# Attention and FFN over half batches, Q and K in rows of three tokens, score units issued in pairs, masks per head pair

## Chip, cores and metric

One core of one Trainium2 chip. The metric is the device time of one execution in microseconds, and medians of several runs are quoted. "Span" is the time from the first to the last instruction in the profile; a run lies some 2 us above its span. The engines are PE (TensorE, matmul), DVE (VectorE), ACT (ScalarE), POOL (GpSimd) and SP (which issues the loads).

## The reference

Four batches, eight heads, 768 tokens, head dimension 64. Heads 0, 2 and 6 are full causal heads. The others see 4 sink tokens and a window of 64. The attention output, 3072 tokens by 512, goes through an FFN.

```python
scores = scale * np.matmul(q, k.transpose(0, 1, 3, 2))        # per batch and head, 768 x 768
mask = causal if retrieval head else causal & (sink | in_window)
a = softmax(where(mask, scores, -1e9))
x = (a @ v) laid out as [B * S, H * D]                        # 3072 x 512
h = np.maximum(np.maximum(x @ w1, x @ w2), x @ w3)            # 3072 x 768
out = h @ w_out                                               # 3072 x 512
```

## The kernel before

It walks over 16 head pairs (two heads, one whole batch of 768 tokens each). For a pair it casts Q and K to 16 bits, transposes them on PE into one PSUM tile, copies them to SBUF, and computes scores in six units. ACT takes the exponential and POOL multiplies by masks. A pair later PE multiplies by V, DVE normalises, and PE transposes the result to become the FFN's input. FFN work for a finished batch is dealt out in small portions ("fill") among the attention of the next batch.

```python
trp = tc.tile_pool(name="trp", bufs=1, space=PSUM)       # ONE transpose buffer
fsp = tc.tile_pool(name="fsp", bufs=2, space=PSUM)       # FFN accumulators
# ... cut ...
retr_row = ...                                           # is_retrieval, one partition
nc.gpsimd.partition_broadcast(out_ap=RT[:, 0:H], in_ap=retr_row[0:1, 0:H])
for h in range(H):                                       # all masks, at the start
    for c, (f, w) in ((0, (full, win)), (256, (full, win)), (512, (full0, win0))):
        nc.vector.scalar_tensor_tensor(out=mk[:, h, c : c + 256], in0=f,
            scalar=RT[:, h : h + 1], in1=w, op0=ALU.mult, op1=ALU.add)
# ... cut ...
def turn(src, nm):                                       # Q or K: [token, dim] -> [dim, token]
    tr = trp.tile([P, 1024], FP16, tag="tr", name="tr")
    for sb in range(NSB):
        nc.tensor.transpose(tr[:, sb * P : (sb + 1) * P],
                            src[:, sb].rearrange("p h d -> p (h d)"), ident)
    t = qkt.tile([P, S], FP16, tag=nm, name=nm)
    nc.vector.tensor_copy(out=t, in_=tr[:, 0:S])
    return t
# turn_x does the same with the normalised output x, into xT, through the same buffer
# ... cut ...
for i in range(NP + 1):
    # ...
    for u in range(6):
        scores(i, u, *cur)                               # conditions cut
        # u = 0..3: av(p, ...) and norm(p, ...) of the pair before
        # u = 2 and u = 4: turn_x(p, 0), turn_x(p, 1)
        # u = 3: nxt[0] = turn(qn, "QT")     u = 5: nxt[1] = turn(kn, "KT")
        fill(RATE)                                       # two FFN units after every score unit
```

Each use of the one transpose buffer is followed by FFN matmuls before the next use.

The softmax here doesn't subtract the row's maximum and nothing guards it: scores larger than these inputs give would overflow.

## Time and profile before

| | before |
|---|---|
| median, range (three runs) | 264.18 us, 261.42 to 264.54 |
| span | 259.6 us |
| first FFN matmul (yy) | 70.8 us |
| stage with attention and FFN | 70.8 to about 226 us |
| FFN alone | about 33.6 us |

The page of the kernel before, its second part: each digit is a tenth of busy time in one fortieth of the span.

```profile
PE   0004675785699999999999999999999999999993
POOL 2006999997997777777677868595959552000000
```

The same in numbers, busy time of each engine by stage (a stretch, its length, then busy time and number of instructions for PE, PE's weight loads, DVE, ACT and POOL, the granted clock, the DMA share and GB/s):

```profile
0.00:70.80 70.80, 33.25 (x318) 19.26 (x319) 43.42 (x81) 25.50 (x28) 49.42 (x59) 1.00 1.23 207
70.80:226.00 155.20, 154.84 (x1502) 85.03 (x1499) 98.78 (x204) 88.44 (x125) 107.86 (x116) 1.00 0.36 80
226.00:259.60 33.60, 29.46 (x155) 14.69 (x152) 11.34 (x21) 8.29 (x16) 0.00 (x0) 1.00 0.13 47
```

Before 70.8 us PE waits. From there it is busy 154.8 of 155.2 us, and at the end the FFN runs alone. The chain of waits (start, length, what) in this stretch of the middle stage is PE alone. Transposes ("tr"), then FFN ("yy"), then the next work: scores ("st") and products with V ("oacc").

```profile
83.71 0.17 PE tr L337 x3
83.88 1.30 PE yy L187 x8
85.18 0.27 PE st L273 x2
85.45 0.58 PE oacc L309 x15
86.03 0.34 PE tr L253 x6
86.36 1.30 PE yy L187 x8
```

The copies that empty the transpose buffer, from the groups of instructions (line, engine, operation, output from input, shapes, count, busy us and mean ns, idle time before):

```profile
L258 DVE COPY KT<-tr 128x768 f16<-128x768 f16 x16 | 8.9, 558 | 5.1 <-PE tr L253 4.3
L341 DVE COPY xT<-tr 128x384 f16<-128x384 f16 x32 | 11.4, 358 | 24.9 <-PE tr L337 24.9
```

So 768 contiguous elements take 0.56 us and 384 take 0.36.

### The profile page before, as it was taken

The numbers are of one execution on the slowest core, as the hardware profiler recorded it, in microseconds if no ns is written. First come the engines' busy times: TensorE is split into PE (matmuls) and PEld (weight loads), VectorE is DVE, ScalarE is ACT, GpSimd is POOL, SyncE is SP. The second block draws the span as 40 slices with busy tenths as digits, with TensorE's granted clock in tenths as the row PEclk, the third lists the DMA queues.
The fourth block names the chain that finished last, engine by engine and source line by source line (L and its number), as shares of the span: only waits on it lengthen the run. The fifth ranks groups of instructions, "written<-read, shape, count | busy, mean of one in ns | idle before, by whom it ended". The sixth has DMA issues, their size and how long they took to land.

```text
span 259.6 us, 4937 instructions
## 1 busy us (share of the span) xinstructions
PE 217.5 (84%) x1968; PEld 119.0 (46%) x1968; DVE 153.5 (59%) x305; ACT 122.2 (47%) x169; POOL 157.3 (61%) x174
## 2 busy tenths in 40 slices
PE   0004675785699999999999999999999999999993
PEld 0003252444355545554555555455645555554541
DVE  1497547675667656774678476847684563551550
ACT  1002744453656575647564756575556654223212
POOL 2006999997997777777677868595959552000000
PEclk9999999999999999999999999999999999999999
DMA  8999999999920079309920991030002001102003
GB/s 152 218 218 218 218 217 195 202 202 218 218 38 0 3 163 260 66 3 185 263 42 3 205 263 20 3 121 3 0 24 102 3 0 71 53 0 93 31 0 121
DMA packets 80344, 28.62 MB, mean 110 GB/s; under 512 B 74946, under 2 KB 77250, under 8 KB 80322
## 3 DMA queue, kind: packets, MB, share of 16 engines
q1 hardware_dynamic: 77954, 25.17, 49.5%
q0 software_dynamic: 2368, 3.15, 6.8%
q8 instruction: 15, 0.25, 0.4%
q14 instruction: 7, 0.06, 0.1%
HBM read 25.17 MB, written 6.29 MB: 121 GB/s over the span
## 4 chain that ended last, share of the span: by engine, by line
PE 69%; DVE 10%; POOL 9%; SPq 5%; DMA 2%; issue 2%; ACT 0%; DVEq 0%; ACTq 0%; POOLq 0%
PE yy L187 34%; PE yo L205 12%; PE oacc L309 9%; PE st L273 7%; POOL pt L284 5%; SPq L103 5%; PE tr L253 4%; DVE qn L234 3%; PE tr L337 3%; POOL vf L240 3%; DMA qs<-in_q_dram 2%; DVE kn L235 2%; DVE va L238 2%; POOL vf L244 1%; DVE acc L198 1%
## 5 line engine op out<-in xcount | busy, mean ns | idle before, releaser
L280 ACT ACTIVATE pt<-st 128x1024 f16<-128x1024 f32 (+1 forms) x96 | 87.4, 919 | 69.9 <-PE st L273 67.1
L284 POOL TENSOR_TENSOR pt<-pt,mk 128x512 f16<-128x512 f16 (+2 forms) x96 | 103.3, 1100 | 23.1 <-ACT pt L280 23.0
L240 POOL TENSOR_SCALAR vf<-va,RT 128x325 f16<-128x325 f16 x32 | 35.5, 1108 | 29.3 <-DVE va L238 27.9
L198 DVE TENSOR_TENSOR acc<-yy,acc 128x384 f16<-128x384 f32 x48 | 26.8, 558 | 37.9 <-PE yy L187 33.2
L195 ACT CAST acc<-yy 128x384 f16<-128x384 f32 x48 | 23.0, 478 | 44.7 <-PE yy L187 44.7
L273 PE MATMUL st<-QT,KT 64*128 64x384 f16 (+2 forms) x288 | 39.3, 330 | 4.5 <-DVE KT L258 3.3
L187 PE MATMUL yy<-xT,w0t 128*128 128x384 f16 x192 | 39.5, 326 | 0.2
L309 PEld LDWEIGHTS <-pt 128*128 128x128 f16 x672 | 27.3, 103 | 26.9 <-issue 10.6
L187 PE MATMUL yy<-xT,w1t 128*128 128x384 f16 x192 | 39.0, 326 | 0.4
L187 PE MATMUL yy<-xT,w2t 128*128 128x384 f16 x192 | 39.0, 326 | 0.0
L309 PE MATMUL oacc<-va,pt 128*128 128x65 f16 x352 | 32.1, 203 | 5.6 <-POOL pt L284 5.5
L205 PE MATMUL yo<-woutt,hT 128*128 128x512 f16 x144 | 34.3, 379 | 0.0
L309 PE MATMUL oacc<-vf,pt 128*128 128x65 f16 x320 | 26.9, 204 | 5.0 <-DVE x L324 5.0
L198 DVE TENSOR_TENSOR hT<-yy,acc 128x384 f16<-128x384 f32 x48 | 26.6, 554 | 3.7 <-PE yy L187 0.6
L253 PE MATMUL tr<-ident,qn 128*128 128x128 f16 x96 | 9.6, 248 | 20.9 <-DVE qn L234 20.9
L341 DVE COPY xT<-tr 128x384 f16<-128x384 f16 x32 | 11.4, 358 | 24.9 <-PE tr L337 24.9
L273 PEld LDWEIGHTS <-KT 64*128 64x128 f16 x288 | 10.9, 97 | 33.0 <-issue 27.6
L187 PEld LDWEIGHTS <-w1t 128*128 128x128 f16 x192 | 18.1, 97 | 11.7 <-issue 1.8
L187 PEld LDWEIGHTS <-w0t 128*128 128x128 f16 x192 | 17.9, 97 | 11.8 <-issue 2.2
L212 ACT COPY ot<-yo 128x512 f32<-128x512 f32 x24 | 14.1, 585 | 18.7 <-PE yo L205 18.7
L187 PEld LDWEIGHTS <-w2t 128*128 128x128 f16 x192 | 17.7, 97 | 10.6
L234 DVE CAST qn<-qs 128x768 f16<-128x768 f32 x16 | 21.0, 1315 | 0.1
(37 smaller groups left out, 151.1 us busy)
## 6 DMA issues: line engine op xcount, KB each, us to landing
qs<-in_q_dram SPq DMA_DIRECT2D x16, 384.0 KB, 6.3
ks<-in_k_dram SPq DMA_DIRECT2D x16, 384.0 KB, 6.4
vs<-in_v_dram SPq DMA_DIRECT2D x16, 384.0 KB, 6.4
out_dram<-ot SPq DMA_DIRECT2D x24, 256.0 KB, 2.4
w0t<-in_moe_w_dram POOLq DMA_DIRECT2D x1, 768.0 KB, 9.7
w1t<-in_moe_w_dram POOLq DMA_DIRECT2D x1, 768.0 KB, 13.1
w2t<-in_moe_w_dram POOLq DMA_DIRECT2D x1, 768.0 KB, 16.9
woutt<-in_moe_w_out_dram POOLq DMA_DIRECT2D x1, 768.0 KB, 21.3
```

The source lines that it names most:

```text
L187: nc.tensor.matmul(yy[:, 0:HALF], w_t[wi][:, ks, ni * P : (ni + 1) * P], xT[b][ks][:, c0 : c0 + HALF], start=(ks == 0), stop=(ks == KS - 1),)
L195: nc.scalar.copy(out=acc, in_=yy[:, 0:HALF])
L198: nc.vector.tensor_tensor(out=dst, in0=yy[:, 0:HALF], in1=acc, op=ALU.max)
L205: nc.tensor.matmul(yo[:, 0:DMdl], hT[ns][:, tb * P : (tb + 1) * P], woutt[:, ns, :], start=(ns == 0), stop=(ns == NNB - 1),)
L212: nc.scalar.copy(out=ot, in_=yo[:, 0:DMdl])
L234: nc.vector.tensor_copy(out=qn, in_=qs.rearrange("p h sb d -> p sb h d"))
L240: nc.gpsimd.tensor_scalar(out=vf[j][:, h, 1:NSB, 0 : D + 1], in0=va[j][:, h, 1:NSB, 0 : D + 1], scalar1=RT[:, h : h + 1], scalar2=None, op ...
L253: nc.tensor.transpose(tr[:, sb * P : (sb + 1) * P], src[:, sb].rearrange("p h d -> p (h d)"), ident,)
L273: nc.tensor.matmul(st[:, hl, c0 : c0 + n], KT[hb : hb + D, ki * P : (ki + 1) * P], QT[hb : hb + D, q0 : q0 + n], start=True, stop=True,)
L280: nc.scalar.activation(out=pt[:, u, :, 0:width], in_=st[:, :, 0:width], func=AF.Exp, scale=sc)
L284: nc.gpsimd.tensor_tensor(out=pt[:, u, :, c0 : c0 + n], in0=pt[:, u, :, c0 : c0 + n], in1=mk[:, 2 * hp : 2 * hp + 2, m0 : m0 + n], op=ALU. ...
L309: nc.tensor.matmul(o[:, qi, hl, 0 : D + 1], pt[:, u, hl, c : c + P], vv[:, 2 * hp + hl, ki, 0 : D + 1], start=(idx == 0), stop=(idx == len ...
```

## The change

The intent: the unit of work becomes a head pair of half a batch, 32 steps in all. FFN work can start earlier and only half a batch is left for the end. Loads are smaller, and Q and K come in rows of three tokens (768 contiguous bytes in place of 256). Score units are issued in pairs. The masks of a head pair are built in the step that needs them, so the first pair need not wait for all. The POOL broadcast at the start becomes a DMA, and the last half batch of FFN may use four PSUM buffers.

The core of the diff, with the kernel before marked by minus; masks' tables, V factors, pool sizes and renamings are cut:

```diff
-                in_=src[b, 2 * hp : 2 * hp + 2].rearrange("h (sb p) d -> p h sb d", p=P),
+                    out=st, in_=src[b, hs, ts].rearrange("h (p j) d -> p h j d", p=P)   # Q, K
@@ masks
-    nc.gpsimd.partition_broadcast(out_ap=RT[:, 0:H], in_ap=retr_row[0:1, 0:H])
+    nc.vector.tensor_copy(out=RT, in_=ir32[:, 0 : 2 * H : 2])       # ir32 loaded to all rows
+    def head_consts(hp):                     # called in the step that prepares pair hp
+        for h in (2 * hp, 2 * hp + 1):
+            for c, f, w in ((256, full0, win0), (0, full, win)):
+                nc.vector.scalar_tensor_tensor(...)
+        nc.vector.tensor_copy(out=fm[:, hs], ...)
@@ turn
-        nc.vector.tensor_copy(out=t, in_=tr[:, 0:S])
+        nc.vector.tensor_copy(               # 128 x (3 x 128): put tokens back in order
+            out=t.rearrange("p (t j) -> p j t", j=HB),
+            in_=tr[:, 0:HALF].rearrange("p (j t) -> p j t", j=HB),
+        )
@@ main loop, one half step
+    FIRST = 7                                # FFN shares begin at step 7
+        scores(s, [0, 1])
+        share(s, 0, 5)                       # a fifth of the step's FFN work
+        av(s - 1)
+        share(s, 1, 5)
+        scores(s, [2, 3])                    # second halves of batches only
+        share(s, 2, 5)
+        turn_x(s - 1)
+        turn(s + 1, 1)                       # K, directly behind turn_x
+        share(s, 3, 5)
+        turn(s + 1, 0)                       # Q
+        prep_v(s + 1)
+        share(s, 4, 5)
```

## The prediction

> **What bounds the kernel now.** Windows cut by stage (span 259.6 us) show three limits.
> (1) 0 to 20.8 us: PE idle. By the timeline POOL's partition broadcast of RT ends only at 10.2, then DVE builds all 24 masks (9.7 us), and only then casts qn, which PE waits for (20.9 us in the waits).
> (2) 20.8 to 70.8: PE busy 33 of 50 us and without FFN work; POOL busy 47.4 of 50. A pair costs POOL about 6.6 us of masks and 3.1 of vf, and DVE's fp32 casts wait in between (one qn cast, 0.77 us median, took 4.45).[...]
> (3) 70.8 to 224: PE busy 152.9 of 153.2, 12.65 us per pair. Then FFN alone to the end: 40 of 192 FFN units, 2.19 us per 12 matmuls although 8 back to back take 1.30 (1.95 per 12): two PSUM buffers are short there.
>
> **What changes, estimated from those durations.**
> - Start: no broadcast, masks per pair (4 x 0.40 us plus fm), loads a third as large. First scores at about 8 instead of 23.8 us; first mask at 11 instead of 28.8. Loads stop binding after the first.
> - Stage 2: seven half steps before FFN. vf falls from 3.1 to about 1.3 us per pair; masks stay about 6.4. But POOL work, casts and the new mask building (about 2.2 us in each of the first steps)[...]: 5 to 6 us per step. First FFN matmul at 46 to 50 instead of 70.8. Weights are issued near 18 instead of 36 and should be there.
> - Stage 3: 168 FFN units (0.65 us each) and 25 half steps of attention. Attention costs PE 4.85 us per pair now; issuing two score units together saves about 0.4. That gives 6.3 us per half step. New cost: turn_x is followed at once by the K transposes in the one tr buffer, so PE waits for the xT copy (0.36 us, about 0.6 from transpose to release, more when an FFN evacuation is ahead of it on DVE); before, FFN work lay between. K to Q, and Q to the next scores, have only one or two FFN units between them and copies of about 0.5 us. I estimate 0.7 to 1.1 us lost per half step: 18 to 28 us in all. This takes back most gain.
> - Tail: one half batch (24 units) instead of 40 units, and four PSUM buffers: 15.6 us of PE plus 4 of last copy and store, against 33.
>
> **Sum.** 48 + 25.5 x 6.3 (161) + 21 + 15.6 + 4[...] = 251 us span; runs lie 2 to 4 above the span, so the steps give about 253. Waits may overlap better than I count: I say 250 us, range 236 to 263. Faster by over 2%: 0.75; within 2%: 0.19; slower: 0.06.
>
> **What would show it.** Right: first yy matmul at 44 to 52 us; PE 80 to 90% busy between there and the tail; the waits list PE tr on DVE xT, some 25 times, 10 us or more in total; tail after the last oacc under 22 us. Wrong: PE above 97% in the middle (then about 232), or first yy after 56.
>
> **What would make it wrong.** The tr waits being hidden (faster); DVE starved by back-to-back POOL masks in steps 0 to 3, or POOL slower on broadcast mask operands (slower); weights landing late.

The recorded sum came to 251 us of span, about 253 for a run; a term of about 1 us is cut from it, so the printed terms add up to 250 (249.6). What the trace shows is a cast that took longer while POOL worked (4.45 us, median 0.77). The 5 to 6 us per step are the author's estimate: they come close to POOL's 3.85 us per half step (half of 1.3 and 6.4) plus the 2.2 of mask building, as if neither ran beside the other, which was not shown. No trace was named for the 0.4 us that paired score units save either.

## The result, and the profile after

The changed kernel takes 281.97 us (280.9 to 282.73, 4 runs) against 264.36 (4 runs) on the same chip. The ratio is 1.068, 95% interval 1.061 to 1.076. Ratios here are the mean time of one kernel's fast runs over that of the other's of the same rounds, so not quite the ratio of the medians. It is clearly slower, and outside the predicted range of 236 to 263.

The page of the changed kernel, the same two rows:

```profile
PE   0333366668888889889898888897788878989994
POOL 2366455444555543455455454446354445253000
```

Busy time by stage; the cuts are the first FFN matmul and the first matmul of the last FFN half:

```profile
0.00:61.40 61.40, 27.50 (x249) 16.23 (x250) 39.51 (x89) 18.51 (x22) 31.79 (x42) 1.00 0.88 203
61.40:261.10 199.70, 171.52 (x1665) 100.85 (x1664) 133.10 (x281) 94.15 (x138) 94.71 (x99) 1.00 0.26 75
261.10:280.80 19.70, 15.74 (x91) 8.70 (x89) 6.70 (x12) 5.22 (x10) 0.00 (x0) 0.99 0.18 67
```

| stage | predicted | measured |
|---|---|---|
| to the first FFN matmul | 48 us | 61.4 us |
| attention and FFN together | 182 us (161 + 21 of waits) | 199.7 us |
| FFN alone, to the end | 15.6 + 4 us | 19.7 us |

The tail came as foreseen in this count; the prediction's own sign, under 22 us after the last "oacc", was missed (257.2 to 280.8, 23.6 us). In the middle stage PE now idles 28 us (199.7 less 171.5), and it idled 0.4 us before. The first stage is only 9 us shorter, although POOL, which held it before, is now busy 31.8 of 61.4 us.

Who waited for whom, the PE lines of the whole span (total us, times, longest); the largest counterpart before was 3.3 us, scores on KT:

```profile
PE tr L297 <- DVE xT L399: 19.1, 30, 1.3
PE st L326 <- DVE QT L306: 13.3, 24, 0.9
PE tr L297 <- DVE KT L306: 11.8, 22, 0.9
```

Of the prediction's own signs two came true in the middle stage, though the kernel got slower: PE busy 80 to 90% (86%), and PE "tr" waiting on xT (24 times, 16.4 us there). The sign against it came too: first yy after 56 us.

The groups for the copies out of the transpose buffer:

```profile
L306 DVE COPY KT<-tr 128x384 f16<-128x384 f16 x32 | 25.6, 801 | 13.7 <-PE tr L297 13.5
L399 DVE COPY xT<-tr 128x384 f16<-128x384 f16 x32 | 11.3, 353 | 16.1 <-PE tr L396 16.1
```

Half as many elements as before take 0.80 instead of 0.56 us, and there are twice as many copies: KT and QT take 51 us of DVE in place of 18. The contiguous xT copy kept its 0.36.

The chain of waits in the middle stage shows PE and DVE taking turns, where in the stretch shown of the kernel before PE stood alone:

```profile
119.86 0.76 PE yy L223 x4
120.62 0.18 PE tr L396 x3
120.80 0.02 issue
120.82 0.37 DVE xT L399
121.19 0.04 issue
121.23 0.34 PE tr L297 x3
121.58 0.02 issue
121.60 0.68 DVE KT L306
122.27 0.04 issue
122.32 0.56 DVE acc L234
122.88 0.75 DVE QT L306
123.63 0.04 issue
123.67 0.61 PE st L326 x8
```

And a step of the first stage, with no FFN work to lay between, again by the chain (lines of "issue", 0.02 to 0.05 us each, left out):

```profile
45.66 1.04 PE st L326 x8
46.69 1.76 PE oacc L371 x30
48.46 0.86 PE st L326 x5
49.34 0.52 PE tr L396 x3
49.88 0.37 DVE xT L399
50.29 0.49 PE tr L297 x3
50.80 0.81 DVE KT L306
51.66 0.49 PE tr L297 x3
52.17 0.81 DVE QT L306
```

This is a serial chain of PE and DVE, 7.4 us per step, with no POOL instruction in it. PE runs slowly here too: the same 30 "oacc" matmuls take 1.76 us in this chain and 0.94 in the middle stage (at 125 us). Why was not shown: the granted clock of the record says 1.00 in both stages.

### The profile page after: what moved, and what is told of

Its sections match the earlier page's. It is cut to its first block, busy times and chain, and to the rows that moved or that the text cites. A ratio compares the mean times of both kernels' runs of the same rounds, so it can differ in the third digit from the quotient of the medians.

```text
span 280.8 us, 5222 instructions
## 1 busy us (share of the span) xinstructions
PE 214.8 (76%) x2000; PEld 125.8 (45%) x2000; DVE 179.3 (64%) x381; ACT 117.9 (42%) x169; POOL 126.5 (45%) x141
## 3 DMA queue, kind: packets, MB, share of 16 engines
q1 hardware_dynamic: 46608, 25.18, 32.1%
## 4 chain that ended last, share of the span: by engine, by line
PE 58%; DVE 27%; issue 5%; ACT 4%; DMA 2%; SPq 2%; POOL 0%; DVEq 0%; ACTq 0%
PE yy L223 21%; PE yy L241 10%; PE st L326 8%; PE oacc L371 7%; PE tr L297 7%; DVE QT L306 5%; DVE KT L306 5%; DVE xT L399 3%; DVE acc L234 3%; ACT pt L334 3%; DVE mk L180 3%; DVE hT L234 3%; PE yst L223 2%; PE tr L396 2%; DVE x L381 1%
## 5 line engine op out<-in xcount | busy, mean ns | idle before, releaser
L356 POOL TENSOR_TENSOR pt<-pt,mk 128x512 f16<-128x512 f16 (+1 forms) x96 | 100.7, 1071 | 56.9 <-ACT pt L334 56.7
L334 ACT ACTIVATE pt<-st 128x1024 f16<-128x1024 f32 x96 | 82.8, 917 | 75.6 <-PE st L326 71.0
L287 POOL TENSOR_TENSOR vf<-va,fm 128x390 f16<-128x390 f16 (+1 forms) x32 | 20.9, 654 | 71.7 <-DVE va L285 71.7
L326 PE MATMUL st<-QT,KT 64*128 64x384 f16 (+2 forms) x320 | 31.2, 309 | 13.7 <-DVE QT L306 13.3
L306 DVE COPY KT<-tr 128x384 f16<-128x384 f16 x32 | 25.6, 801 | 13.7 <-PE tr L297 13.5
L297 PE MATMUL tr<-ident,kn 128*128 128x128 f16 x96 | 11.7, 238 | 27.9 <-DVE xT L399 19.1
L306 DVE COPY QT<-tr 128x384 f16<-128x384 f16 x32 | 25.5, 798 | 10.5 <-PE tr L297 10.5
L241 PE MATMUL yy<-woutt,hT 128*128 128x512 f16 x132 | 31.8, 379 | 0.0
L248 ACT COPY ot<-yy 128x512 f32<-128x512 f32 x22 | 12.9, 588 | 26.2 <-PE yy L241 23.4
L297 PEld LDWEIGHTS <-kn 128*128 128x128 f16 x96 | 8.6, 105 | 32.1 <-issue 23.0
```

Source lines behind the costliest of these rows:

```text
L241: nc.tensor.matmul(yo[:, 0:DMdl], hT[ns][:, tb * P : (tb + 1) * P], woutt[:, ns, :], start=(ns == 0), stop=(ns == NNB - 1),)
L248: nc.scalar.copy(out=ot, in_=yo[:, 0:DMdl])
L287: nc.gpsimd.tensor_tensor(out=vf[j][:, hs, k0:k1, 0 : D + 1], in0=va[j][:, hs, k0:k1, 0 : D + 1], in1=fm[:, hs, k0:k1], op=ALU.mult,)
L297: nc.tensor.transpose(tr[:, j * P : (j + 1) * P], src[:, j].rearrange("p h d -> p (h d)"), ident)
L306: nc.vector.tensor_copy(out=t.rearrange("p (t j) -> p j t", j=HB), in_=tr[:, 0:HALF].rearrange("p (j t) -> p j t", j=HB),)
L326: nc.tensor.matmul(st[:, hl, c0 : c0 + n * P], KT[hb : hb + D, ki * P : (ki + 1) * P], QT[hb : hb + D, q0 * P : (q0 + n) * P], start=True, ...
```

## The experiments

Theory A: the loss is waiting between PE and DVE around the one transpose buffer, and reordering copies of 0.80 us make those waits long. Theory B: DVE and POOL are overloaded or hold each other up (as the cast of 4.45 us beside POOL suggests), and if one wait is mended another takes its place. A third question is whether half batches are themselves the loss. Each kernel is the changed one with the edit shown, unless said otherwise. Times are medians of four runs; the kernel before took 262.6 to 264.0 in these rounds. The changed kernel was not run again in them, and differences are taken from its 281.97; as the kernel before moved by over a microsecond from round to round, total differences under about 2 us are not resolved.

### 1. One token per row, contiguous copy

```diff
-                    out=st, in_=src[b, hs, ts].rearrange("h (p j) d -> p h j d", p=P)
+                    out=st[:, hl], in_=src[b, 2*hp + hl, ts].rearrange("(j p) d -> p j d", p=P)  # per head
-            out=t.rearrange("p (t j) -> p j t", j=HB), in_=tr[...].rearrange("p (j t) -> p j t", j=HB)
+            out=t, in_=tr[:, 0:HALF]
```

> Q and K loaded with one token per row again, so that the copy out of PSUM is contiguous; all else as in the changed kernel (282 us). Theory A (the loss is in waits between PE and DVE around the one transpose buffer, made long by the reordering copies of 0.80 us): KT and QT copies fall to 0.36 us, each of the seven steps before FFN gets about 0.9 us shorter (first yy at about 55 instead of 61.4), the stage after it loses another 10 to 13 us, total about 263. Theory B (DVE and POOL are loaded[...], the waits on PE only show it): the stage with FFN shortens by less than 4 us, total above 273. Loads get slower with 256 byte rows; if loading mattered, the first yy would not come earlier.

Measured: 268.3 us, ratio 1.015. The copies take 0.36 us, and the first yy comes at 55.3. 14 us are gone: for A, though less than the 19 expected. By the profiles 6.1 us of it lie before the first yy and 9.4 in the middle stage (now 190.3 us), where 10 to 13 were expected. The longest wait, that on xT, did not move (19.6). Loads took longer with rows of 256 bytes in the kernel before: the packets of the main DMA queue, 25.2 MB in each, took 49.5% of 16 engines' 259.6 us before and 32.1% of 280.8 in the changed kernel, where of the loads only V keeps such rows (39.9% of 257.7 in run 8, with the rows of before).

### 2. Two halves of the transpose buffer in turn

```diff
+    tr_both = trp.tile([P, 1024], FP16, tag="tr", name="tr")     # allocated once
-        tr = trp.tile([P, 1024], FP16, tag="tr", name="tr")
+        tr = tr_both[:, c : c + 512]                             # c = 0, 512 in turn
```

> The one transpose buffer is used as two halves in turn, reordering copies kept at 0.80 us. Theory A: the waits of PE transposes on the xT copy (19.1 us) and on the KT copy (11.8 us) nearly vanish, those of the score matmuls on QT stay; total about 257 to 262, of which about 5 us before the first yy. Theory B: other waits take their place, total above 273.

Measured: 281.51 us, no change, and the wait is the same to the tenth:

```profile
PE tr L306 <- DVE xT L408: 19.1, 30, 1.3
```

This looks like a verdict for B, but it is none. In the trace the first K transpose still carries a semaphore wait, and starts 0.05 us after the xT copy ends: in the program as built, the two halves did not count as two buffers. The run therefore tests nothing. A separate second buffer was not tried.

### 3. x transposes one FFN share earlier

```diff
+            turn_x(s - 1)
         share(s, 2, 5)
-            turn_x(s - 1)
```

> The transposes of x are issued one FFN share earlier, so that FFN matmuls lie between them and the K transposes; same instructions, same buffers. Theory A: in the stage with FFN the wait on the xT copy (16.4 us there) falls to below 4 us; the first yy stays at 61.4; total about 268 to 270. Theory B: total above 277.

Measured: 270.78 us, ratio 1.025; the middle stage takes 188.7 us in place of 199.7. The wait on the xT copy fell from 19.1 to this, for the whole span:

```profile
PE tr L297 <- DVE xT L399: 3.6, 8, 0.5
```

The same instructions in another order, two lines apart, are worth 11 us. That is what A says and B excludes; the run missed its range of 268 to 270 by 0.8. In the middle stage PE idled 18.5 us in place of 28.2; a part came back as a wait on x (3.4 us, none before). The first yy came at 60.1 instead of 61.4 although nothing before it was changed, so this reading varies by about a microsecond.

### 4. Masks built once

Wrong result; it reads the first pair's masks for all pairs.

```diff
-        if s < NHP:
+        if s < 1:
             head_consts(hp)
```

> Wrong result on purpose: masks and V factors are built for the first head pair alone and used for all, so the building leaves three of the first four steps. If the building sits on the chain of those steps (four mask operations of 1.64 to 2.57 us and 0.34 for fm, three times), first yy comes 6 to 8 us earlier and the total is about 274 to 276. If the first steps hang on PE transposes and copies or on POOL alone, less than 3 us.

Measured: 276.74 us, 5.2 less; first yy at 56.4, 5.0 earlier. The building is on the chain of the first steps, at a little less than expected.

### 5. FFN work from step 5

```diff
-    FIRST = 7
+    FIRST = 5
```

> The changed kernel with the FFN work let in from step 5 instead of step 7 and spread over 28 instead of 26 steps; nothing else. If steps 5 and 6 are a chain of PE and DVE with PE mostly waiting (first yy at 61.4 us, 7.4 us per step), about 12 FFN units (7.8 us of PE) move there and partly fill the waits[...]: first yy at about 46 us, total 274 to 277. If these steps are bound by POOL, DVE or the loads, the FFN work only lengthens them: 280 or more.

Measured: 275.55 us, ratio 1.048; first yy at 46.9. PE was waiting in those steps (busy 7.1 of the 11.4 us from 50.0 to 61.4 in the changed kernel), and work put there is partly free: 6.4 us less in total.

### 6. Edits 1 and 3 together

> One token per row with contiguous copies, and the x transposes one share earlier, together. Alone they took off 14 and 11 us. If they cut different waits, the total is 256 to 259, clear below the kernel before (264); if they share the same waits, above 262. Left in the stage with FFN should be under 8 us of PE waits on DVE copies.

Measured: 255.2 us, ratio 0.970 (0.962 to 0.978). Alone the edits took 13.7 and 11.2 us, together 26.8: they mend different waits (255.2 is 0.8 below the expected range). The changed kernel is now faster than the one before. The middle stage takes 177.0 us, and PE idles 9.7 in it.

### 7. Edits 1, 3 and 5, and casts in another order

```diff
-        nc.vector.tensor_copy(out=kn, in_=ks_.rearrange("p h j d -> p j h d"))
+        nc.vector.tensor_copy(out=kn.rearrange("p j h d -> p h j d"), in_=ks_)     # Q likewise
```

> As the one before, and with FFN work from step 5, and with the K and Q casts written in the order of the loaded tile (outer dimension 2 instead of 3), which should take them from 0.54 to about 0.34 us like the V cast of the same size. Expected 246 to 252: another 5 us from FFN work in steps 5 and 6, 1 to 4 from the casts that stand in the chain of the first steps. If the half batch walk were itself the loss, it would stay above 258.

Measured: 251.42 us, ratio 0.956. This is inside the expected range. Half batches are not the loss.

### 8. The kernel before with an early start alone

The kernel before, with is_retrieval loaded to all partitions and the masks built per pair behind the V cast.

> The kernel before with one part of the change alone: is_retrieval loaded to all partitions by the DMA, no POOL broadcast, masks built per head pair when the pair is prepared; whole batches kept. First scores at about 11 instead of 23.8 us, first POOL mask at about 16 instead of 28.8, the POOL bound first stage (10 us per pair) unchanged, first yy at about 58 instead of 70.8, the rest as before: total 251 to 255. If the first stage is held by the loads instead (DMA nearly always busy until 70 us), less than 4 us is gained.

Measured: 258.13 us, ratio 0.982 (0.974 to 0.990), less than half of the gain expected. First yy at 66.9 instead of 58. The chain shows what was overlooked: at the start of the kernel before, POOL idle, 24 mask operations took 9.7 us, so six take 2.4. Here six took 3.0 us for the first pair and 8.6 for the fourth.

```profile
8.55 3.01 DVE mk L154 x6
...
38.22 8.57 DVE mk L154 x6
```

POOL was busy beside both: beside the first pair with V factors alone, beside the fourth with V factors and mask products. One operation makes most of the difference. The last of the six began at 41.9 and took 4.88 us (median 0.61), over nearly the whole of four mask products that POOL did back to back:

```profile
L154 DVE SCALAR_TENSOR_TENSOR mk<-full,RT,win x24: 470/614/4883, 8.5 to 41.9; 128x256 f16<-128x256 f16 x24
42.66 4.64 POOL L286 TENSOR_TENSOR pt<-pt,mk 128x512 f16<-128x512 f16 x4
```

So the mask building, moved out of the start where POOL was idle, took longer beside POOL; by what mechanism was not shown. (The profiled run also had a granted clock of 0.69 between 40 and 67 us, so this one page does not show how much of the late first yy the mask building alone made.)

### 9. Contiguous copy, rows of three tokens kept

Wrong result: tokens of Q and K stay permuted. The comparison with the reference still passed, probably because with inputs this small (0.1 times a normal distribution) the attention is nearly even over the tokens it sees; the order is wrong all the same. So the comparison does not catch a wrong order of Q and K tokens; for the other runs that order rests on reading the code.

```diff
-            out=t.rearrange("p (t j) -> p j t", j=HB), in_=tr[...].rearrange("p (j t) -> p j t", j=HB)
+            out=t, in_=tr[:, 0:HALF]
```

> Wrong result on purpose (tokens of Q and K stay in the order of the loads): the changed kernel with three tokens per row kept, but the copy out of PSUM contiguous. It parts the two halves of the run with one token per row (268 us). If the copy alone was the cost, KT and QT copies take 0.36 us and the total is 265 to 269, first yy at about 55; below 265 by as much as the longer rows help. If the one-token rows did it, the total stays above 277.

Measured: 264.62 us, ratio 1.006 (0.996 to 1.016); first yy at 55.1. So of edit 1 the copy did the work: 17 us. What the longer rows give is the difference to run 1, 3.7 us by the medians with overlapping intervals (1.007 to 1.022 there), so not settled. By the profiles the first yy differs by 0.2 us and the middle stage by 1.2.

### 10. Reordering on the reading side

```diff
-            out=t.rearrange("p (t j) -> p j t", j=HB), in_=tr[...].rearrange("p (j t) -> p j t", j=HB)
+            out=t.rearrange("p (t j) -> p t j", j=HB), in_=tr[...].rearrange("p (j t) -> p t j", j=HB)
```

> The changed kernel, correct, with the reordering done on the reading side: the copy walks PSUM with a stride of 128 elements and writes SBUF contiguously, instead of reading contiguously and writing every third element. If the 2-byte writes with a stride make the 0.80 us, the copy takes 0.36 to 0.55 and the total 270 to 276; if any reordering of 2-byte elements costs that, it stays at 0.80 and the total at 280 to 282.

Measured: 272.3 us, ratio 1.036, correct.

```profile
L306 DVE COPY KT<-tr x32: 556/556/559, 7.8 to 236.9; 128x384 f16<-128x384 f16 x32
```

The line gives the shortest, median and longest copy in ns. The same permutation costs 0.56 us when the stride is on the reading side and 0.80 when every third element is written; contiguous it is 0.36. Ten microseconds for exchanging two letters on both sides.

The middle stage of runs 10 and 9, to be read beside the 199.70 and 171.52 of the changed kernel:

```profile
57.00:251.00 194.00, 171.99 (x1665) 100.86 (x1664) 125.33 (x282) 94.14 (x138) 94.84 (x100) 0.99 0.26 77
55.10:244.20 189.10, 168.69 (x1665) 100.20 (x1664) 116.72 (x282) 94.13 (x138) 94.96 (x100) 0.99 0.27 79
```

PE idles 28.2 us there with copies of 0.80 us, 22.0 with 0.56 and 20.4 with 0.36.

### 11. The casts alone

The cast edit of run 7 on the changed kernel.

> The changed kernel with only the order of the K and Q casts changed (outer dimension 2 instead of 3). [...]they fall from 0.54 to 0.34 us as the V cast, except where they wait for POOL. The casts are on the chain only in the first four steps, so the total falls by 1 to 3 us at most (278 to 281)[...].

Measured: 280.37 us, which the noise does not separate from the changed kernel (ratio 1.067, 1.060 to 1.074, against 1.068). The medians fell to 0.35 us for both casts, from 0.54. The Q cast's mean stayed at 0.54, the longest being 1.06: in the trace 15 of the 32 take 0.56 or 1.05 us, each beside a vf operation of POOL of about 0.45 or 0.94. In the changed kernel none took over 0.55. So, as expected, the form of 0.35 us is held up beside POOL at times; what that costs or gains in total is too small to see here. The condition under which the expectation put its 0.34 us, and its last clause, are cut: no trace shows what makes one form faster.

### 12. Transposes parted by FFN shares

Edits 1 and 5, and the order K, x, Q with a share after each:

```diff
+            turn(s + 1, 1)
         share(s, 2, 5)
             turn_x(s - 1)
-            turn(s + 1, 1)
         share(s, 3, 5)
```

> The version meant to beat both: one token per row, contiguous copies, FFN work from step 5, and the three groups of transposes each parted by an FFN share in the order K, x, Q. In the run with all mends the PE waits left were 13.4 us on x and 10 on the K and Q copies; the wait on x should fall below 5 us outside the first steps. Expected 243 to 248 us against about 263 before. If it stays at 251, those waits were covered by others.

Measured: 243.25 us, ratio 0.925 (0.919 to 0.931). It is correct, and the fastest version. By stage:

```profile
0.00:42.30 42.30, 17.57 (x142) 9.79 (x142) 29.24 (x73) 11.12 (x14) 24.73 (x34) 1.00 0.93 179
42.30:222.20 179.90, 175.02 (x1770) 102.87 (x1769) 129.65 (x297) 101.08 (x146) 102.37 (x107) 1.00 0.44 110
```

The middle stage holds two more steps than that of the changed kernel, and PE is busy 175.0 of its 179.9 us. DVE is no less busy than in the changed kernel, 72% against 67% of the stage, and yet PE waits for it only 2.7 us there (on xT, six times): its load was not the trouble.

## Why the prediction was wrong

By the terms of its sum: the span of 280.8 us is 31 above the 250 that the printed terms add up to. 13.4 of it lie in the first stage (61.4 against 48), 10.5 in PE's work in the middle (171.5 against 161), 7.2 in PE's waits there (28.2 against 21), and nothing in the tail.

- **Bounds of the kernel before: right.** Three stages, PE full in the middle.
- **Tail: right**, 19.7 us against 19.6, counted from the first matmul of the last FFN half.
- **The waits in the middle: their kind right, their size wrong.** The prediction named "PE waits for the xT copy" behind turn_x, and K to Q and Q to scores. All three are in the waits, and run 3 shows the first to be worth 11 us. The step that failed here is **"copies of about 0.5 us"**. They measured 0.80, because the copy writes every third 2-byte element, and nothing in the profile of before had that form. With copies of 0.56 us, nearly as assumed, PE idled 22.0 us (run 10): the 21 of the sum was sound for the copies it assumed. Run 9 puts the price of the reordering at 17 us of total, of which 10.6 in this stage (199.7 to 189.1; 7.8 of idle and 2.8 of busy time) and 6.3 before it. But this step alone does not explain the miss: with copies of 0.56 us the kernel still took 272.3 us.
- **The first stage: its size and its cause wrong.** The step that failed is **"5 to 6 us per step"**, estimated as if POOL work, casts and the new mask building held each other up, and with it the first FFN matmul at 46 to 50. It came at 61.4. POOL was busy half of the stage and is not in the chain. What can be put down to waiting beside POOL on that chain is small: the four mask buildings took 1.64, 2.22, 2.57 and 1.64 us, 1.5 more than four times the shortest. The steps (7.4 us each at the end) were held by a serial chain of PE at nearly half its speed (1.76 us in place of 0.94 for 30 "oacc" matmuls), copies, and in the first four steps mask building. Runs 9 and 4 take 6.3 and 5.0 us off it, which together would end at about 50 (an estimate, the two were not run together). How much the slow PE added was not tested alone. From the durations of one such step, scores, oacc and transposes take 5.1 us there against about 3 in the middle stage, so an estimate of 2 us for each of the three heaviest steps.
- **PE's work in the middle: too small.** The step that failed is **"6.3 us per half step"** (161 us). It comes out only if the 0.4 us that paired score units save is taken off every half step: 168 x 0.65 / 25.5 = 4.3 of FFN and 4.85 / 2 = 2.4 of attention make 6.7, less 0.4. Without any saving these figures give 171 us, and PE was busy 171.5. After edits 1 and 3, with most waits gone, it was still busy 167.3 of 177.0. So the work was taken 6 us or more too small. The 0.4 was the author's estimate, and what the paired units save was not tested alone.
- **"Waits may overlap better than I count" was a hope.** No trace was named for it. That hope, and a chance of 0.75 for faster, stood against an own sum of 253 that was within 5% of no gain.
- **Rival B is out.** Run 3 moved nothing but the order and took 11 us; run 12 brought PE to 97% in the middle stage at no lower DVE load. DVE operations held up beside POOL show in run 8 (4.88 us, median 0.61) and run 11 (casts of 0.56 and 1.05, median 0.35) but do not explain this result.

Left open: what a true second transpose buffer would give (run 2 did not make one), what the rows of three tokens are worth by themselves, and what the slow PE of the first stage and the paired score units each cost or save.

## What to carry to other kernels

When an engine is full, look in the new program order for every place where it needs back a buffer that another engine must first empty, and lay independent work between. Here two lines exchanged were worth 11 us of 282. A layout chosen for the load is paid for where it is undone: cost the reordering copy by a measured copy with the same strides, not by one with the same size (here 0.80 us against 0.36). And before moving work from an idle start to the place where it is needed, see what it meets there (in run 8, 8.6 us in place of 2.4).
